# Two-input subtractions to VectorE, casts to GpSimd, in an attention and gated-convolution kernel on one Trainium2 core

## The chip, the cores and the metric

The kernel runs on one core of a Trainium2 chip. A core has a matrix engine (TensorE, PE in the rows), a vector engine (VectorE, DVE), a scalar engine (ScalarE, ACT), a general engine (GpSimd, POOL) and an engine that issues transfers (SyncE, SP). They run at the same time, each through its own list of instructions in order, and wait for one another on semaphores. The metric is the device time of the whole program in microseconds (us), as the median of several runs.

## The reference

The inputs are q, k and v (4 batches, 8 heads, 768 positions, head width 64) and the weights of a feed-forward block (512 to 1024 and back). First comes attention with a bias that falls with distance, over the last 96 positions and the first 8 ones:

```python
scores = np.matmul(q, k.transpose(0, 1, 3, 2)) / np.sqrt(D) - slopes * dist
scores = np.where(is_global | is_local, scores, -1e9)
a = softmax(scores)                       # over the keys, with 1e-9 in the denominator
x = (a @ v).transpose(0, 2, 1, 3).reshape(B, S, H * D)
```

Then a feed-forward block with a gate from a convolution of three taps along the sequence:

```python
h = np.maximum(x @ w_in, 0.0)
c = sum(conv_w[t] * shifted(h, t) for t in range(3))
out = (h * sigmoid(c)) @ w_out
```

Everything is float32, but the weights and the convolution's taps come in as 64-bit floats.

## The kernel before, in words

**Units, jobs and steps.** A unit is one batch and one half of the sequence (384 positions): 8 units. Each has 4 jobs, one for each pair of heads (32 jobs, m = 0 to 31), and each job has 3 steps, one for each block of 128 queries (96 steps, s = 0 to 95). A step makes the scores of both heads (`scores`), their maxima (`maxima`, one instruction on VectorE per head that adds the table of biases, L419), the exponentials (`exps`, ScalarE, L431), and two steps later the transposes on TensorE and their copy by ScalarE (`transposes`, L463 to L470). After the last step of a job come the product with v (`values`, L479), the scaling by the sum's inverse (`mixed`: L492 on VectorE, then a split) and the input x of the feed-forward block.

**Two-part products.** The large products use a rounded float32 format (fp32r). To keep accuracy, an operand a is split: a high part is the cast of a to fp32r, and a low part is a minus the high part, also in fp32r. This happens to k and q (`prep`, from job 5 on; jobs 0 to 4 use plain float32), to the weights (`weight_high`, `weight_low`), to x (`mixed`) and to the gated activations (`split`). A cast reads one operand, a subtraction two. Which engine does which is what the change is about. Before: casts of k and q are on ScalarE in the early jobs and on VectorE later, casts of x, weights and gated activations on ScalarE; subtractions are on GpSimd, with listed exceptions on VectorE.

**Names.** In the rows `kk` holds both parts of k (the upper 64 partitions become the low part), `qh` and `ql` those of q, `xh` and `xl` those of x, `wih`, `wil`, `woh`, `wol` those of the two weight matrices, `gh` and `gl` those of the gated activations. `rk`, `rq` are k and q as loaded, `wr` is a raw weight piece, `w` a decoded one, `hbuf` holds h, `c` the convolution.

**Feed-forward.** `ffn(n)` lists the work of unit n: products with w_in (`mm1`), the convolution (`conv`: one tap on GpSimd, L561, two on VectorE, L562 and L563), the tanh of the gates, `split`, and the products with w_out of the unit before (`mm2`). `fill` deals this list out over the 12 steps of the next unit, so attention of one unit and the block of an earlier one share the engines. A unit of even number has 56 such products in its list, an odd one 40.

**Weights.** 16 pieces are turned from 64-bit to 32-bit floats by three instructions on VectorE each (`weight_bits`, L318, L320, L322), then cast, then subtracted. Small lists of chores (`chores`) hold this work; at each step `work` takes from a list until its budget in us for the step is spent (DECODE_BY_HAND, DECODE_LATER). `need` finishes pieces at once when a product wants them.

**Order.** The first 11 steps (HAND) are recorded in the order of the code. From then on a scheduler that simulates the engines sets the order on each engine, bounded by `issue_after`. After the last product, `check_weights` and `check_gates` look for inputs that would need the slower general path; that path isn't run here.

## Time and profile before

| | |
|---|---|
| median of 3 runs | 520.48 us (520.05 to 522.03) |
| the profiled execution's own time | 522.24 us |
| its span, first to last instruction | 520.5 us |
| busy: TensorE, VectorE, ScalarE, GpSimd | 467.4, 381.5, 310.8, 281.5 us |
| granted TensorE clock, mean | 0.951 |

The times of instructions in the prediction come from the profiled execution. A row of groups gives line, engine, operation, output and inputs, count, then the busy time and the mean of one in ns, then the engine's idle time just before these instructions and what ended it. A row of a timeline gives start and duration in us. Two instructions of one engine can overlap by some hundredths of a microsecond, so the sum of durations is a little more than the busy time.

### The profile page before, as it was taken

Reading aid. Unit: us, or ns where it says so; the run is one execution under the profiler, and the core shown is the slowest. Engines: PE = TensorE matmul, PEld = TensorE weight load, DVE = VectorE, ACT = ScalarE, POOL = GpSimd, SP = SyncE. Lnnn points to the kernel's source line nnn. Section 1 sums busy time; section 2 is a strip of 40 time slices with the busy share of each in tenths; the row PEclk is TensorE's granted clock in tenths of the full one; section 3 lists DMA queues with packets and bytes.
Section 4 is the critical chain, followed back from the end, with each engine's and each line's share of the span. In section 5 each row is a group of like instructions: output and inputs, shape, how many; then the busy total and the mean of one; then the engine's idle time right before and its main releaser. Section 6 shows DMA issues by size and latency. Waiting matters only on the chain.

```text
span 520.5 us, 8853 instructions
## 1 busy us (share of the span) xinstructions
PE 467.4 (90%) x3109; PEld 397.7 (76%) x3109; DVE 381.5 (73%) x825; ACT 310.8 (60%) x825; POOL 281.5 (54%) x242
## 2 busy tenths in 40 slices
...
GB/s 187 258 202 211 150 217 105 94 93 124 104 99 61 120 94 63 76 141 127 88 122 110 87 87 94 131 128 110 101 101 122 52 67 57 55 224 210 168 60 47
DMA packets 22965, 61.78 MB, mean 119 GB/s; under 512 B 3072, under 2 KB 4608, under 8 KB 22912
## 3 DMA queue, kind: packets, MB, share of 16 engines
...
q8 instruction: 26, 0.43, 0.3%
...
## 4 chain that ended last, share of the span: by engine, by line
PE 40%; DVE 32%; ACT 10%; DMA 8%; issue 5%; POOL 2%; SPq 1%; ACTq 0%; POOLq 0%; DVEq 0%
PE o L625 17%; PE h L512 8%; DVE c L562 6%; PE pv L479 6%; DVE c L563 4%; DVE s L419 4%; PE s L400 4%; DVE c L613 3%; DMA check<-in_w_out 3%; DMA check<-in_w_in 2%; DVE kk L136 2%; ACT pbuf L431 2%; DVE w L322 2%; PE t L463 2%; DVE w L318 2%
## 5 line engine op out<-in xcount | busy, mean ns | idle before, releaser
L431 ACT ACTIVATE pbuf<-s,mm 128x232 f32<-128x232 f32 (+1 forms) x192 | 82.7, 437 | 81.1 <-DVE mm L419 73.4
L419 DVE CUSTOM_DVE_ANT_0 s<-s,tab 128x232 f32<-128x232 f32 (+1 forms) x192 | 72.9, 387 | 34.5 <-PE s L400 27.1
L625 PE MATMUL o<-woh,gh 128*128 128x512 f32 x192 | 79.4, 413 | 2.6 <-ACT gh L614 2.3
L561 POOL TENSOR_SCALAR c<-hbuf,cw 128x382 f32<-128x382 f32 (+1 forms) x64 | 51.5, 811 | 53.0 <-ACT hbuf L525 38.8
L625 PE MATMUL o<-wol,gh 128*128 128x512 f32 x192 | 77.0, 401 | 0.0
L625 PE MATMUL o<-woh,gl 128*128 128x512 f32 x192 | 76.7, 400 | 0.0
L479 PE MATMUL pv<-pt,v 104*64 104x128 f32 (+2 forms) x768 | 63.0, 294 | 13.3 <-issue 5.4
L143 POOL TENSOR_TENSOR kk<-rk,kk 64x1008 fp32r<-64x1008 f32 (+1 forms) x27 | 61.8, 2289 | 18.3 <-POOL ql L145 6.2
L145 POOL TENSOR_TENSOR ql<-rq,qh 128x768 fp32r<-128x768 f32 x24 | 48.8, 2034 | 37.4 <-DVE qh L140 25.5
L479 PEld LDWEIGHTS pv<-pt,v 104*64 104x64 f32 (+2 forms) x768 | 44.9, 142 | 31.3 <-issue 14.5
L562 DVE SCALAR_TENSOR_TENSOR c<-hbuf,cw,c 128x382 f32<-128x382 f32 (+1 forms) x64 | 57.1, 903 | 15.7 <-POOL c L561 15.5
L512 PE MATMUL h<-xh,wih 128*128 128x384 f32 x252 | 61.4, 361 | 6.4 <-ACT xh L493 4.7
L563 DVE SCALAR_TENSOR_TENSOR c<-hbuf,cw,c 128x382 f32<-128x382 f32 (+1 forms) x64 | 61.7, 972 | 0.6
L463 PE MATMUL t<-ident,pbuf 128*128 128x128 f32 (+1 forms) x192 | 51.1, 290 | 9.7 <-ACT pt L470 3.1
L512 PE MATMUL h<-xl,wih 128*128 128x384 f32 x252 | 58.9, 347 | 0.0
L512 PE MATMUL h<-xh,wil 128*128 128x384 f32 x252 | 55.1, 340 | 0.0
L400 PE MATMUL s<-kk,qh 128*128 128x232 f32 (+1 forms) x162 | 44.2, 295 | 10.8 <-ACT pbuf L431 10.8
L470 ACT ACTIVATE pt<-t 128x512 f32<-128x512 f32 x80 | 47.4, 595 | 9.9 <-PE t L464 8.2
L512 PEld LDWEIGHTS h<-xh,wih 128*128 128x128 f32 x252 | 45.9, 200 | 9.0 <-ACT xh L493 5.1
L616 POOL TENSOR_TENSOR gl<-c,gh 128x1024 fp32r<-128x1024 f32 (+2 forms) x16 | 36.3, 2276 | 26.6 <-ACT gh L614 20.2
L464 PE MATMUL t<-ident,pbuf 128*128 128x128 f32 x192 | 49.6, 282 | 0.4 <-POOL pbuf L282 0.4
L494 POOL TENSOR_TENSOR xl<-rs,xh 128x384 fp32r<-128x384 f32 x32 | 36.9, 1154 | 20.7 <-ACT xh L493 16.4
...
## 6 DMA issues: line engine op xcount, KB each, us to landing
...
```

The costliest lines, as they stand in the source:

```text
L143: G.tensor_tensor(kk[64:], rk[64:], kk[64:].bitcast(F32), ALU.subtract)
L400: last_mm[s] = T.matmul(sp[j][:, c0 : c0 + n], q_[:, j * TB + i * P : j * TB + (i + 1) * P], kk[:, j * w + k0 : j * w + k0 + n], start=st, ...
L419: last_ttr[s] = V.tensor_tensor_reduce(out=sp[j][:, c0 : c0 + n], in0=sp[j][:, c0 : c0 + n], in1=tb, scale=-0.125, scalar=3.0e38, op0=ALU. ...
L431: last_exp[s] = A.activation(pb[:, j, c0 : c0 + n], sp[j][:, c0 : c0 + n], AF.Exp, bias=mm[:, j : j + 1], scale=-1.0, accum_out=sums[m][:, ...
L463: T.transpose(pt[:ka, j, 0, :], pb[:, j, c0:P], ident)
L464: T.transpose(pt[:, j, 1, :], pb[:, j, P:256], ident)
L479: T.matmul(pv[m][64 * j : 64 * j + 64, i * P : (i + 1) * P], vt[m][:n, i, c, 64 * j : 64 * j + 64], sb[:n, j, c, :], start=c == 0, stop=c ...
L512: T.matmul(ps[:, :TB], w_[:, k, fs], x_, start=part == 0 and k == 0, stop=part == 2 and k == NK - 1,)
L561: G.tensor_scalar(c, *tap(1), 1.0, ALU.mult, ALU.mult)
L562: V.scalar_tensor_tensor(c, *tap(0), c, ALU.mult, ALU.add)
L563: V.scalar_tensor_tensor(c, *tap(2), c, ALU.mult, ALU.add)
L625: T.matmul(ps, g_[:, f], w_[:, f], start=f == 0 and part == 0, stop=f == NF - 1 and part == 2,)
```

## The change

All subtractions that make a low part (of k, q, x, the weights and the gated activations) are now on VectorE. The casts that make the high parts of k, q, x and the weights are on GpSimd; the cast of the gated activations stays on ScalarE. The chores have no list for ScalarE any more: GpSimd's list gets the cast of a weight piece in the step in which its last bits are decoded, and VectorE's list gets the subtraction three places behind the front. The budgets of VectorE's list are changed, and it comes ahead of GpSimd's.

```diff
--- before.py
+++ after.py
@@ -38,12 +38,8 @@
 NATIVE = 5
 WARM = (43, 0, 16, 16, 16, 12, 8, 4, 4, 4, 4, 4)
 EARLY = 1
-K_ON_ACT, Q_ON_ACT = 13, 10
-Q_LOW_ON_DVE = (10, 12, 14)
-W_LOW_ON_DVE = (14,)
 RELU_ON_DVE = (0, 2, 2)
-SPLIT_ON_DVE = (1,)
-DECODE_BY_HAND, DECODE_LATER = (0.7, 0.4, 0.6), (0.6, 1.2)
+DECODE_BY_HAND, DECODE_LATER = (0.3, 1.2, 1.4), (1.2, 1.2)
 FIRST_LOADS = (0, 0, 1, 2)
 SHARE = (0.3, 0.5)
 AT = ((2, 4, 5, 9, 16, 25), (1, 2, 4, 6, 7, 12, 16))
@@ -130,19 +126,12 @@
             ql = p2.tile([P, 2 * TB], F32R, tag="ql", name=f"ql{m}")
             kk = p2.tile([P, 2 * w], F32R, tag="kk", name=f"kk{m}")
             qk[m] = (qh, ql, kk)
-            if m < K_ON_ACT:
-                A.activation(kk, rk, AF.Copy)
-            else:
-                V.tensor_copy(kk, rk)
-            if m < Q_ON_ACT:
-                A.activation(qh, rq, AF.Copy)
-            else:
-                V.tensor_copy(qh, rq)
+            G.tensor_copy(kk, rk)
+            G.tensor_copy(qh, rq)
         else:
             qh, ql, kk = qk[m]
-            G.tensor_tensor(kk[64:], rk[64:], kk[64:].bitcast(F32), ALU.subtract)
-            X = V if m in Q_LOW_ON_DVE else G
-            X.tensor_tensor(ql, rq, qh.bitcast(F32), ALU.subtract)
+            V.tensor_tensor(kk[64:], rk[64:], kk[64:].bitcast(F32), ALU.subtract)
+            V.tensor_tensor(ql, rq, qh.bitcast(F32), ALU.subtract)
 
     manual = tc.manual_schedule()
     manual.__enter__()
@@ -324,14 +313,13 @@
     def weight_high(i, half):
         t = wt[i, half]
         h, l = weight_planes(i)
-        A.activation(h[:, half * HF : (half + 1) * HF], t, AF.Copy)
+        G.tensor_copy(h[:, half * HF : (half + 1) * HF], t)
 
     def weight_low(i, half):
         t = wt[i, half]
         h, l = weight_planes(i)
         sl = slice(half * HF, (half + 1) * HF)
-        X = V if i * 2 + half in W_LOW_ON_DVE else G
-        X.tensor_tensor(l[:, sl], t, h[:, sl].bitcast(F32), ALU.subtract)
+        V.tensor_tensor(l[:, sl], t, h[:, sl].bitcast(F32), ALU.subtract)
 
     def check_weights():
         width = -(-NK * FF // NCHK)
@@ -490,8 +478,8 @@
         xt[m] = (xh, xl)
         x = rs.pop(m)
         V.tensor_tensor(x, pv[m], x, ALU.mult)
-        cur["mixed"] = A.activation(xh, x, AF.Copy)
-        G.tensor_tensor(xl, x, xh.bitcast(F32), ALU.subtract)
+        G.tensor_copy(xh, x)
+        cur["mixed"] = V.tensor_tensor(xl, x, xh.bitcast(F32), ALU.subtract)
 
     def ends(s):
         return s >= 0 and s % NB == NB - 1
@@ -612,8 +600,7 @@
         else:
             V.scalar_tensor_tensor(c, c, 1.0, h, ALU.add, ALU.mult)
         A.activation(gh[:, :, sl], c, AF.Copy)
-        X = V if n % 2 in SPLIT_ON_DVE and n > 1 else G
-        X.tensor_tensor(gl[:, :, sl], c, gh[:, :, sl].bitcast(F32), ALU.subtract)
+        V.tensor_tensor(gl[:, :, sl], c, gh[:, :, sl].bitcast(F32), ALU.subtract)
 
     def mm2(b, t, f):
         gh, gl = gt[b, t]
@@ -708,7 +695,7 @@
                 fn(*a)
                 k -= cost
 
-    chores = {"dve": [], "act": [], "pool": []}
+    chores = {"dve": [], "pool": []}
 
     def work(eng, budget):
         q = chores[eng]
@@ -724,12 +711,12 @@
     def piece_bits(i, half, n):
         weight_bits(i, half, n)
         if n == 2:
-            chores["act"].append((cur["s"] + 1, 0.5, piece_high, (i, half)))
+            chores["pool"].append((cur["s"], 0.7, piece_high, (i, half)))
             free_slot((i, half))
 
     def piece_high(i, half):
         weight_high(i, half)
-        chores["pool"].append((cur["s"] + 1, 1.2, piece_low, (i, half)))
+        chores["dve"].insert(3, (0, 0.56, piece_low, (i, half)))
 
     def piece_low(i, half):
         weight_low(i, half)
@@ -737,7 +724,7 @@
 
     def need(*pieces):
         while not all(p in done for p in pieces):
-            for q in ("pool", "act", "dve"):
+            for q in ("pool", "dve"):
                 if chores[q]:
                     _, _, fn, args = chores[q].pop(0)
                     fn(*args)
@@ -786,8 +773,8 @@
             if s in (4, 6):
                 conv_weights((s - 4) // 2)
             budget = DECODE_BY_HAND[min(s // 3, len(DECODE_BY_HAND) - 1)]
-            for eng in ("pool", "act", "dve"):
-                work(eng, budget if eng == "dve" else 1.3)
+            work("dve", budget)
+            work("pool", 1.3)
         else:
             if hand:
                 hand = False
@@ -823,9 +810,8 @@
             if s < len(steps):
                 budget = DECODE_LATER[min((s - HAND) // 3, len(DECODE_LATER) - 1)]
                 with tc.issue_after(last_ttr[s].ins):
+                    work("dve", budget)
                     work("pool", 1.2)
-                    work("act", 0.9)
-                    work("dve", budget)
         if s == 0:
             for k in range(len(order)):
                 chain(*order[k])
```

Since lines are taken out, the line numbers of the changed kernel are up to 14 lower: L407 is the maximum (L419 before), L133 and L134 are the subtractions of k and q, L129 and L130 their casts, L307, L309 and L311 the three decoding instructions, L322 the subtraction of a weight piece, L480 the scaling of x (L492 before), L481 and L482 its cast and subtraction, L550 and L551 two taps, L603 the subtraction of the gates.

**First place: VectorE in the steps 6 to 8**, which are in the order of the code. Before (a row `ISA s7...` is a maximum of step 7, and `mm7` is where it is put):

```order
L492 TENSOR_TENSOR rs0_400<-pv0_383,rs0_400 128x384
L439 TENSOR_SCALAR sums1_306<-sums1_306 128x6
L440 RECIPROCAL sums1_306<-sums1_306 128x6
L255 SCALAR_TENSOR_TENSOR setup_84<-setup_84 128x24
L256 TENSOR_TENSOR cw_187<-cw_187,setup_84 128x24
L322 SCALAR_TENSOR_TENSOR w2_0_429<-wr2_0_252,w2_0_429 128x512
L419 ISA s7_0_477,mm7_487<-s7_0_477,tab_169 128x232
L419 ISA mm7_487 128x1
L419 ISA s7_1_476,mm7_487<-s7_1_476,tab_169 128x232
L419 ISA mm7_487 128x1
L318 TENSOR_SCALAR w3_0_499<-wr3_0_292 128x512
L320 SCALAR_TENSOR_TENSOR w3_0_499<-wr3_0_292,w3_0_499 128x512
```

And now, from the same instruction (the scaling of x for job 0) on:

```order
L480 TENSOR_TENSOR rs0_403<-pv0_386,rs0_403 128x384
L482 TENSOR_TENSOR xl0_456<-rs0_403,xh0_455 128x384
L427 TENSOR_SCALAR sums1_301<-sums1_301 128x6
L428 RECIPROCAL sums1_301<-sums1_301 128x6
L244 SCALAR_TENSOR_TENSOR setup_84<-setup_84 128x24
L245 TENSOR_TENSOR cw_187<-cw_187,setup_84 128x24
L322 TENSOR_TENSOR wil_189<-w1_0_329,wih_188 128x512
L309 SCALAR_TENSOR_TENSOR w3_0_435<-wr3_0_287,w3_0_435 128x512
L311 SCALAR_TENSOR_TENSOR w3_0_435<-wr3_0_287,w3_0_435 128x512
L407 ISA s7_0_485,mm7_495<-s7_0_485,tab_169 128x232
L407 ISA mm7_495 128x1
L407 ISA s7_1_484,mm7_495<-s7_1_484,tab_169 128x232
```

The subtraction for x of job 0 (`xl0`) and one of a weight piece stand ahead of the maxima of step 7, and piece `w3_0` is fully decoded there; before, its decoding began behind those maxima.

**Second place: VectorE between the maxima of step 29 and step 30**, where the scheduler sets the order. Before:

```order
L563 SCALAR_TENSOR_TENSOR c0_839<-hbuf_192,cw_187,c0_839 128x382
L419 ISA s29_1431,mm29_1436<-s29_1431,tab_169 128x232
L419 ISA mm29_1436 128x1
L140 CAST qh11_1537<-rq11_1428 128x768
L439 TENSOR_SCALAR sums9_1334<-sums9_1334 128x6
L419 ISA s30_1487,mm30_1492<-s30_1487,tab_169 128x136
L419 ISA mm30_1492 128x1
L440 RECIPROCAL sums9_1334<-sums9_1334 128x6
```

And now:

```order
L601 SCALAR_TENSOR_TENSOR c0_856<-c0_856,hbuf_192 128x8x128 x2
L133 TENSOR_TENSOR kk10_1382<-rk10_1280,kk10_1382 64x816
L427 TENSOR_SCALAR sums9_1334<-sums9_1334 128x6
L603 TENSOR_TENSOR gl0_0_1446<-c0_856,gh0_0_1445 128x1024
L428 RECIPROCAL sums9_1334<-sums9_1334 128x6
L134 TENSOR_TENSOR ql10_1381<-rq10_1281,qh10_1380 128x768
L603 TENSOR_TENSOR gl0_1_1519<-c0_856,gh0_1_1518 128x1024
L482 TENSOR_TENSOR xl7_1340<-rs7_1311,xh7_1339 128x384
L480 TENSOR_TENSOR rs8_1467<-pv8_1450,rs8_1467 128x384
L133 TENSOR_TENSOR kk11_1539<-rk11_1427,kk11_1539 64x816
L407 ISA s30_1487,mm30_1492<-s30_1487,tab_169 128x136
L407 ISA mm30_1492 128x1
```

Six subtractions (for k of jobs 10 and 11, q of job 10, x of job 7, and two tiles of the gates) and five other instructions now stand between these two maxima; before there was a cast, and an addition for the sums.

**Third place: the steps 58 and 59**, in an odd unit in the middle of the run. VectorE before:

```order
L562 SCALAR_TENSOR_TENSOR c3_2693<-hbuf_192,cw_187,c3_2693 128x386
L419 ISA s58_2956,mm58_2961<-s58_2956,tab_169 128x232
L419 ISA mm58_2961 128x1
L562 SCALAR_TENSOR_TENSOR c3_2693<-hbuf_192,cw_187,c3_2693 128x386
L563 SCALAR_TENSOR_TENSOR c3_2693<-hbuf_192,cw_187,c3_2693 128x386
L419 ISA s58_2956,mm58_2961<-s58_2956,tab_169 128x232
L419 ISA mm58_2961 128x1
L563 SCALAR_TENSOR_TENSOR c3_2693<-hbuf_192,cw_187,c3_2693 128x386
L140 CAST qh21_3091<-rq21_2995 128x768
L419 ISA s59_2998,mm59_3003<-s59_2998,tab_169 128x232
L419 ISA mm59_3003 128x1
L136 CAST kk21_3093<-rk21_2994 128x1008
```

VectorE now:

```order
L133 TENSOR_TENSOR kk20_2949<-rk20_2842,kk20_2949 64x1008
L407 ISA s58_2956,mm58_2961<-s58_2956,tab_169 128x232
L407 ISA mm58_2961 128x1
L482 TENSOR_TENSOR xl17_2914<-rs17_2873,xh17_2913 128x384
L407 ISA s58_2956,mm58_2961<-s58_2956,tab_169 128x232
L407 ISA mm58_2961 128x1
L550 SCALAR_TENSOR_TENSOR c3_2693<-hbuf_192,cw_187,c3_2693 128x386
L551 SCALAR_TENSOR_TENSOR c3_2693<-hbuf_192,cw_187,c3_2693 128x386
L407 ISA s59_2998,mm59_3003<-s59_2998,tab_169 128x232
L407 ISA mm59_3003 128x1
L550 SCALAR_TENSOR_TENSOR c3_2693<-hbuf_192,cw_187,c3_2693 128x386
L407 ISA s59_2998,mm59_3003<-s59_2998,tab_169 128x232
```

The two casts (of q and k for job 21) are gone from here, and two subtractions (k of job 20, x of job 17) came in. GpSimd in the same place, before:

```order
L145 TENSOR_TENSOR ql20_2948<-rq20_2843,qh20_2947 128x768
L143 TENSOR_TENSOR kk20_2949<-rk20_2842,kk20_2949 64x1008
L445 COPY wide18_2920<-sums18_2747 128x384
L494 TENSOR_TENSOR xl17_2914<-rs17_2873,xh17_2913 128x384
L561 TENSOR_SCALAR c3_2693<-hbuf_192,cw_187 128x386 x3
L145 TENSOR_TENSOR ql21_3092<-rq21_2995,qh21_3091 128x768
L143 TENSOR_TENSOR kk21_3093<-rk21_2994,kk21_3093 64x1008
```

GpSimd now:

```order
L130 CAST qh20_2947<-rq20_2843 128x768
L129 CAST kk20_2949<-rk20_2842 128x1008
L481 CAST xh17_2913<-rs17_2873 128x384
L549 TENSOR_SCALAR c3_2693<-hbuf_192,cw_187 128x386
L433 COPY wide18_2920<-sums18_2747 128x384
L549 TENSOR_SCALAR c3_2693<-hbuf_192,cw_187 128x386
L130 CAST qh21_3091<-rq21_2995 128x768
L549 TENSOR_SCALAR c3_2693<-hbuf_192,cw_187 128x386
L129 CAST kk21_3093<-rk21_2994 128x1008
```

Each two-input subtraction of that list has become a one-input cast of the same tile; the taps of the convolution and the copy `wide` stay.

## The prediction

> **What bounds the kernel now.** First the busy times, then the shares of the chain of waits by engine:

> ```profile
> PE 467.4 (90%) x3109; PEld 397.7 (76%) x3109; DVE 381.5 (73%) x825; ACT 310.8 (60%) x825; POOL 281.5 (54%) x242
> PE 40%; DVE 32%; ACT 10%; DMA 8%; issue 5%; POOL 2%; SPq 1%; ACTq 0%; POOLq 0%; DVEq 0%
> ```

> PE looks full, but its chain share is only 40%, and DVE has 32%. The table of stretches (us; PE, PEld, DVE, ACT, POOL busy; granted clock; DMA share; GB/s) shows where each rules:

> ```profile
> 16.00:60.00 44.00, 38.59 (x304) 28.30 (x304) 35.13 (x96) 29.56 (x89) 29.32 (x25) 0.88 0.63 204
> 60.00:115.00 55.00, 37.03 (x248) 31.70 (x247) 47.37 (x95) 35.59 (x93) 36.97 (x30) 0.84 0.39 137
> 115.00:177.00 62.00, 53.38 (x349) 45.63 (x349) 53.44 (x96) 40.74 (x106) 44.22 (x28) 0.91 0.33 102
> 242.00:292.00 50.00, 46.74 (x337) 40.26 (x337) 43.85 (x88) 30.34 (x87) 29.27 (x24) 1.00 0.36 111
> 292.00:354.00 62.00, 62.00 (x413) 55.11 (x412) 44.80 (x96) 39.30 (x104) 36.75 (x29) 0.97 0.32 100
> 354.00:404.00 50.00, 46.74 (x338) 40.25 (x337) 43.35 (x88) 30.91 (x88) 29.14 (x24) 1.00 0.36 111
> 454.00:521.00 67.00, 55.66 (x257) 45.87 (x256) 29.03 (x69) 27.59 (x64) 7.96 (x9) 0.97 0.47 143
> ```

> Three regimes. In the ramp (16 to 177) DVE is the busiest engine or near it, PE idles and its clock is down to 0.84. Then two kinds of unit alternate: one with PE without a gap (62.00 of 62), one of 50 us with PE idle for 3.3 us while DVE is 87% busy. The tail from 454 on hardly uses POOL.

> Much of DVE's busy time is waiting. In the timeline, a cast alone and one beside a POOL subtraction:

> ```profile
> 256.76 0.68 DVE L136 CAST kk<-rk 128x1008 fp32r<-128x1008 f32 x1
> 268.51 0.55 DVE L140 CAST qh<-rq 128x768 fp32r<-128x768 f32 x1
> 269.19 1.84 POOL L145 TENSOR_TENSOR ql<-rq,qh 128x768 fp32r<-128x768 f32 x1 [1.86 <-PE rt L453]
> 269.30 2.28 DVE L136 CAST kk<-rk 128x1008 fp32r<-128x1008 f32 x1
> 271.50 0.61 DVE L562 SCALAR_TENSOR_TENSOR c<-hbuf,cw,c 128x386 f32<-128x386 f32 x1
> ```

> The cast of 0.68 us took 2.28: it ended 0.55 after the POOL subtraction did (269.19 + 1.84 = 271.03), so it stood still meanwhile. The groups say how common that is:

> ```profile
> L562 DVE SCALAR_TENSOR_TENSOR c<-hbuf,cw,c 128x382 f32<-128x382 f32 (+1 forms) x64 | 57.1, 903 | 15.7 <-POOL c L561 15.5
> L563 DVE SCALAR_TENSOR_TENSOR c<-hbuf,cw,c 128x382 f32<-128x382 f32 (+1 forms) x64 | 61.7, 972 | 0.6
> L613 DVE SCALAR_TENSOR_TENSOR c<-c,hbuf 128x1024 f32<-128x1024 f32 x20 | 32.3, 1632 | 2.9 <-ACT sat L592 2.9
> L136 DVE CAST kk<-rk 128x1008 fp32r<-128x1008 f32 x11 | 18.7, 1698 | 0.0
> L136 DVE CAST kk<-rk 128x816 fp32r<-128x816 f32 x8 | 14.8, 1846 | 0.0
> L140 DVE CAST qh<-rq 128x768 fp32r<-128x768 f32 x22 | 15.0, 680 | 13.7 <-PE s L400 11.9 <-DMA rq<-in_qk 1.7
> L318 DVE TENSOR_SCALAR w<-wr 128x512 int32<-128x512 int32 x16 | 14.5, 904 | 2.1 <-DMA wr<-in_w_in 2.1
> L320 DVE SCALAR_TENSOR_TENSOR w<-wr,w 128x512 int32<-128x512 int32 x16 | 14.8, 937 | 0.2
> L322 DVE SCALAR_TENSOR_TENSOR w<-wr,w 128x512 int32<-128x512 int32 x16 | 16.2, 1015 | 0.0
> L616 DVE TENSOR_TENSOR gl<-c,gh 128x1024 fp32r<-128x1024 f32 x9 | 11.0, 1219 | 4.3 <-ACT gh L614 4.3
> L492 DVE TENSOR_TENSOR rs<-pv,rs 128x384 f32<-128x384 f32 x32 | 17.1, 535 | 10.0 <-ACT rs L455 9.9
> 12.77 0.43 DVE L318 TENSOR_SCALAR w<-wr 128x512 int32<-128x512 int32 x1 [2.11 <-DMA wr<-in_w_in]
> 13.23 0.69 DVE L320 SCALAR_TENSOR_TENSOR w<-wr,w 128x512 int32<-128x512 int32 x1
> ```

> Mean less undisturbed duration gives the stall. Taps: (903 + 972 - 2 x 610) x 64 = 42 us. L613 against the 1.22 of L616 (same size): 20 x 0.41 = 8 us. Weights: 16 x (0.47 + 0.25 + 0.33) = 17 us. Casts of k: 33.5 us against at most 19 x 0.68 = 13, so 20 us or more. Together 87 us of DVE's 381.5 are stall.

> **The change part by part.** POOL loses these groups:

> ```profile
> L143 POOL TENSOR_TENSOR kk<-rk,kk 64x1008 fp32r<-64x1008 f32 (+1 forms) x27 | 61.8, 2289 | 18.3 <-POOL ql L145 6.2
> L145 POOL TENSOR_TENSOR ql<-rq,qh 128x768 fp32r<-128x768 f32 x24 | 48.8, 2034 | 37.4 <-DVE qh L140 25.5
> L616 POOL TENSOR_TENSOR gl<-c,gh 128x1024 fp32r<-128x1024 f32 (+2 forms) x16 | 36.3, 2276 | 26.6 <-ACT gh L614 20.2
> L494 POOL TENSOR_TENSOR xl<-rs,xh 128x384 fp32r<-128x384 f32 x32 | 36.9, 1154 | 20.7 <-ACT xh L493 16.4
> L334 POOL TENSOR_TENSOR wil<-w,wih 128x512 fp32r<-128x512 f32 x8 | 12.0, 1500 | 4.3 <-ACT wih L327 4.1
> L334 POOL TENSOR_TENSOR wol<-w,woh 128x512 fp32r<-128x512 f32 x7 | 9.6, 1378 | 1.8 <-ACT woh L327 1.8
> ```

> That is 205 us. It gains 102 casts, which the trace of before doesn't show on POOL. The nearest one-input rows:

> ```profile
> 263.13 0.50 POOL L445 COPY wide<-sums 128x384 f32<-128x384 f32 x1 [1.35 <-DVE sums L440]
> L218 POOL TENSOR_SCALAR tab<-setup 128x232 bf16<-128x232 f32 x2 | 0.8, 387 | 0.2
> 265.45 1.88 POOL L561 TENSOR_SCALAR c<-hbuf,cw 128x386 f32<-128x386 f32 x2 [0.27 <-ACT hbuf L525]
> 266.33 0.62 DVE L562 SCALAR_TENSOR_TENSOR c<-hbuf,cw,c 128x386 f32<-128x386 f32 x1
> 266.87 0.87 DVE L563 SCALAR_TENSOR_TENSOR c<-hbuf,cw,c 128x386 f32<-128x386 f32 x1
> ```

> From 387 ns at 232 to 500 at 384 a line rises by 0.74 ns an element: 0.79 us for q (768), 0.96 and 0.82 for k (1008, 816), 0.60 for a weight piece, 0.50 for x. Sum: 27 x 0.79 + 15 x 0.96 + 12 x 0.82 + 16 x 0.60 + 32 x 0.50 = 71 us. Below, every cast costs the 0.50 of the smallest (51 us). Above, each cast costs what the removed subtraction of the same tile did: 61.8 for k, 27 x 2.03 for q, 16 x 1.44 for weights, 36.9 for x, 177 us. I take 71, since a cast is nearest to a copy. POOL then falls to about 150 us. ACT loses the casts of x, weights and early k, q: fewer instructions, none of them ahead of anything new.

> DVE gains 114 subtractions. Between the rows of 535 ns at 384 and 1219 at 1024, a line gives 0.68, 0.95, 1.00 and 1.20 us at 512, 768, 816 and 1008. Sum: 15 x 1.20 + 12 x 1.00 (k) + 24 x 0.95 (q) + 15 x 0.68 (weights) + 32 x 0.54 (x) + 15 x 1.22 (gates) = 98 us, less 0.08 of overlap each (the cast at 269.30 ran to 271.58, the next began at 271.50): 89 us. It loses its casts, 48.5 us with their stalls, and the other stalls, 67 us.

> New stalls are the disputed cost. Removed: 87 us of stall for 205 us of subtraction, 0.42 per us. Beside a one-input POOL instruction the tap at 266.33 took 0.62 (free) and that at 266.87 took 0.87 (0.26 stall), while POOL's pair took 1.88, where two such copies would take 1.0: here POOL waited more than DVE. Bounds: 0.26 us at one cast in three, 9 us; or 0.42 x 71 = 30 us. I take 20. DVE: 381.5 - 48.5 - 67 + 89 + 20 = 375 us, by the bounds 364 to 385.

> So DVE is no emptier, but no instruction waits 1.6 us at a time.

> A wait is added: a subtraction on DVE now waits for POOL's cast, and behind it stand the next step's maxima, for which ACT's exponentials wait (in the first place of the order, `xl0` ahead of step 7). If POOL is in a tap of the convolution just then, that is up to 0.5 us more, once a job for x; k and q are prepared a job ahead and are hidden by the steps of the running job. With POOL at 150 of 520 us this meets fewer than a third of 32 jobs, 5 us of DVE, half of it in units that PE fills; it is inside the new stall's bounds. By stretch:

> Units of the 50 us kind: 16 of 128 taps (5.3 us of stall), four casts of k (4.2), three of L613 (1.2) lose 10.7; the casts at free speed go (4 x 0.68 + 4 x 0.55, less overlap, 4.3); in come 4 x (1.20 + 0.95 + 0.54) less overlap, 9.8, and new stall, 2.5. Net -2.7 in each, with PE's idle 3.3 as the ceiling. There are two and a quarter of them: **-6 us**, between 0 and -7.5. In units of 62 us PE has no gap: **0**.

> Ramp: DVE's sum is a draw there, but POOL leaves the chain where these stood in it:

> ```profile
> 134.88 4.66 POOL gl L616 x2
> 139.60 2.39 POOL kk L143
> ```

> 7.05 us become two subtractions of 1.14 and one of 1.12 on DVE: **-4 us**, between 0 (DVE has 8.6 us free in 62 there) and -12 (if weights, now ready sooner behind one another on DVE, also cut waits between 60 and 115). The early steps get more: up to the maxima of step 10 five more decoding instructions (2.5 us), four weight subtractions (2.4) and two of x (0.9), 5.8 us; I take that as repaid later, since decoding is ahead by then. **0**, up to +6.

> Tail: no moved instruction of it is on POOL before but three tiles of the gates: **0**.

> Sum: 522.24 (the profiled execution, 1.74 beyond its span) - 10 = 512. It lies 1.76 over the median of 520.48, so against the runs shown: **510.5 us**.

> **The rivals.**

> *No change.* The 50 us units are also tied by the loop from maxima to exponentials, where ACT waits for DVE. The subtractions are put between the maxima of two steps, as casts were; if this loop sets the pace, the 2.7 is kept out of the time, and the ramp draws: 520. For: DVE has 6 us of idle there even now. Against: the stalls sit directly on the chain.

> *Slower by the ramp.* DVE is at 80 and 86% from 16 to 115. The 5.8 us ahead of step 10 are not repaid, and between the maxima of steps 29 and 30 six subtractions add 0.92 x 2 + 1.14 x 2 + 0.87 + 0.46 = 5.4 us where PE waits for k and q of job 10: 522.24 + 5.8 + 5.4 - 4 (of the steady gain) - 1.76 = 527. It decides from the point where DVE is above some 92% in 16 to 60 (35.1 + 5.8 of 44 is 93%).

> *Slower by the lock.* POOL's casts stop DVE as the subtractions did, and 89 us more of two-input work can be stopped: 0.42 x 71 x 1.4 = 42 us of stall, 22 more than taken. Over 500 us, 2.2 in each 50 us unit (the gain falls to 1) and 7 in the ramp: 510.5 + 5 + 7 = 522; with casts at the subtractions' price (177 us) 0.42 x 177 = 74, 54 more, and about 535. I put the middle, 529. [...]

> *Much faster.* Waits of PE in the ramp (18 us idle from 60 to 115) go too, since a weight's subtraction takes 0.60 instead of 1.4 to 1.5: -12 there and -7: 501.

> **How the numbers follow.** Forecast 0.49 (own range 504 to 517), no change 0.18, slower by the ramp 0.16, by the lock 0.08, much faster 0.09. A measurement here tells 0.5% (2.6 us) from nothing: faster 0.58, same 0.18, slower 0.24. The range goes from 499 to 527, which leaves out the far ends of the lock and of the much faster case.

> **What would show it.** Right: taps near 0.65 us in the mean, POOL's casts at 0.5 to 1.0, DVE busy 364 to 385, POOL about 150, units of 47 to 48 us. Wrong: taps still at 0.8 and more (the lock), casts over 1.3, DVE over 92% busy from 16 to 60 and the same maxima later (the ramp), or PE gaps in the units that had none.

## The result, and the profile after

The changed kernel takes 498.27 us in the median of 4 runs (495.63 to 501.8), beside 521.25 us (520.05 to 522.44) for the kernel before: the ratio is 0.956, with an interval of 0.950 to 0.963. Its profiled execution took 495.63 us, its span is 493.9 us. The forecast was 510.5 us, with 499 to 527 as its range: the direction was right, and the gain was more than twice the forecast one. Ratios and their intervals leave out slow executions (over 1.5% above the fastest of the same kernel) and can differ from the quotient of the medians given.

Busy times and the chain of waits of the changed kernel:

```profile
PE 461.4 (93%) x3109; PEld 395.6 (80%) x3109; DVE 379.3 (77%) x898; ACT 279.9 (57%) x764; POOL 181.1 (37%) x230
PE 73%; DVE 13%; DMA 7%; ACT 3%; issue 1%; SPq 0%; POOL 0%; DVEq 0%; ACTq 0%; POOLq 0%
```

VectorE is as busy as before (379.3 against 381.5 us), but its share of the chain fell from 32% to 13%, and TensorE's rose from 40% to 73%. Whatever was won was not won in VectorE's sum.

The same stretches as in the prediction, of the changed kernel (columns as there):

```profile
16.00:60.00 44.00, 37.02 (x278) 26.88 (x279) 40.05 (x114) 19.77 (x69) 19.88 (x27) 0.84 0.73 231
60.00:115.00 55.00, 41.99 (x266) 36.68 (x264) 48.77 (x111) 27.92 (x83) 28.97 (x30) 0.82 0.37 119
115.00:177.00 62.00, 59.59 (x415) 51.11 (x415) 56.74 (x120) 39.87 (x109) 27.58 (x31) 0.99 0.34 108
242.00:292.00 50.00, 50.00 (x356) 44.16 (x352) 41.40 (x96) 31.79 (x88) 21.14 (x25) 1.00 0.37 114
292.00:354.00 62.00, 62.00 (x443) 54.55 (x442) 47.25 (x112) 38.44 (x107) 24.73 (x29) 1.00 0.35 110
```

From 16 to 60 TensorE did less than before (278 matmuls against 304) while VectorE was busier (40.05 against 35.13). From 115 to 177 it did 415 against 349, at a clock of 0.99 against 0.91. In the last two stretches it has no gap.

Stretches of equal time hold different work, so from here on both kernels are cut at equal work: at the start of the first maximum of steps 12, 48 and 95, read from the records of that instruction (each step has two; of those of the changed kernel, L407, 96 start before 208.2 us, from 7.9 to 206.5 us, which is steps 0 to 47). First the kernel before, then the changed one:

```profile
0.00:38.10 38.10, 32.48 (x302) 25.20 (x304) 25.95 (x96) 20.77 (x70) 18.01 (x42) 0.96 0.72 212
38.10:221.70 183.60, 153.56 (x1005) 130.38 (x1000) 153.20 (x295) 117.54 (x305) 126.96 (x90) 0.89 0.35 116
221.70:436.70 215.00, 208.39 (x1439) 182.39 (x1439) 168.14 (x357) 136.24 (x371) 121.27 (x98) 0.99 0.33 101
436.70:520.50 83.80, 72.96 (x374) 59.72 (x370) 34.21 (x81) 36.24 (x82) 15.27 (x14) 0.98 0.42 127
```

```profile
0.00:40.00 40.00, 36.36 (x306) 28.06 (x307) 31.54 (x106) 18.04 (x63) 15.13 (x43) 0.91 0.75 218
40.00:208.20 168.20, 148.44 (x998) 127.23 (x997) 148.24 (x329) 96.52 (x269) 80.38 (x84) 0.92 0.39 123
208.20:412.50 204.30, 204.30 (x1434) 180.14 (x1432) 159.94 (x380) 129.25 (x355) 78.26 (x92) 1.00 0.34 106
412.50:493.90 81.40, 72.35 (x376) 60.12 (x374) 39.56 (x89) 36.10 (x79) 7.34 (x11) 0.99 0.42 131
```

This is the whole account, for this pair of executions. Steps 0 to 11 got 1.9 us longer, steps 12 to 47 got 15.4 us shorter, steps 48 to 94 got 10.7 us shorter, and the end 2.4 us: 26.6 us of span. The medians differ by 23.0 us, and a second profiled execution of the changed kernel (500.3 us of span, below) lies 20.2 us under that of before; half of what it takes longer is in its first 12 steps. In the long ramp (steps 12 to 47) VectorE's busy time fell by only 5.0 us (153.2 to 148.2) and its idle time by 10.4 (30.4 to 20.0); TensorE's idle time fell by 10.2 (30.0 to 19.8) and its busy time, at a clock of 0.92 instead of 0.89, by 5.1. In the steady part TensorE had 6.6 us of gaps (215.0 - 208.4) and has none; GpSimd's busy time fell from 121 to 78.

The groups of the changed kernel that answer to those of the prediction (mean of one in ns behind the bar):

```profile
L550 DVE SCALAR_TENSOR_TENSOR c<-hbuf,cw,c 128x386 f32<-128x386 f32 x32 | 22.2, 703 | 1.7 <-POOL c L549 1.6
L551 DVE SCALAR_TENSOR_TENSOR c<-hbuf,cw,c 128x386 f32<-128x386 f32 x32 | 22.7, 722 | 0.3
L601 DVE SCALAR_TENSOR_TENSOR c<-c,hbuf 128x1024 f32<-128x1024 f32 x20 | 26.9, 1366 | 7.2 <-ACT sat L580 7.2
L134 DVE TENSOR_TENSOR ql<-rq,qh 128x768 fp32r<-128x768 f32 x27 | 28.0, 1037 | 0.1
L130 POOL CAST qh<-rq 128x768 fp32r<-128x768 f32 x27 | 26.4, 977 | 65.6 <-PE s L388 59.4 <-DMA rq<-in_qk 6.1
L129 POOL CAST kk<-rk 128x1008 fp32r<-128x1008 f32 x15 | 19.3, 1287 | 11.7 <-DMA rk<-in_qk 6.9 <-issue 2.4 <-PE s L378 2.4
L129 POOL CAST kk<-rk 128x816 fp32r<-128x816 f32 x12 | 16.2, 1347 | 8.0 <-DMA rk<-in_qk 8.0
L481 POOL CAST xh<-rs 128x384 fp32r<-128x384 f32 x32 | 23.5, 734 | 57.6 <-DVE rs L480 57.4
```

The taps fell from 903 and 972 ns to about 700 and 720, and L601 (L613 before) from 1632 to 1366. GpSimd's casts take some 98 us in all (these rows, and 7.1 + 5.7 for the weights). Adding up, over VectorE's records, duration less undisturbed duration of the same form, the stall on VectorE fell from 104 to 31 us. The two sums depend on which durations are called undisturbed (with the shortest of each form they are 134 and 62); their difference, 72 to 73 us, hardly does.

How a stall became a gap of TensorE in the ramp of the kernel before, in its timeline just ahead of step 39 (GpSimd, VectorE, TensorE), and behind it the stretches of windows (columns as above):

```profile
167.80 2.83 POOL L143 TENSOR_TENSOR kk<-rk,kk 64x1008 fp32r<-64x1008 f32 x1 [5.28 <-DVE kk L136]
168.35 4.62 DVE L613 SCALAR_TENSOR_TENSOR c<-c,hbuf 128x16 f32<-128x16 f32 x3
172.98 5.31 POOL L616 TENSOR_TENSOR gl<-c,gh 128x1024 fp32r<-128x1024 f32 x2 [1.08 <-ACT gh L614]
173.22 3.02 DVE L613 SCALAR_TENSOR_TENSOR c<-c,hbuf 128x1024 f32<-128x1024 f32 x1
176.17 0.54 DVE L492 TENSOR_TENSOR rs<-pv,rs 128x384 f32<-128x384 f32 x1
176.81 1.51 PE L479 MATMUL pv<-pt,v 128*64 128x128 f32 x10 [5.42 <-issue]
...
171.40:176.80 5.40, 0.00 (x0) 0.02 (x1) 5.40 (x7) 4.39 (x10) 4.32 (x3) 0.93 0.38 138
176.80:180.20 3.40, 3.39 (x19) 2.41 (x20) 1.68 (x6) 1.82 (x6) 3.08 (x3) 0.50 0.20 77
180.20:183.60 3.40, 3.40 (x15) 3.40 (x16) 0.93 (x4) 1.56 (x5) 2.02 (x2) 0.61 0.00 0
```

A subtraction for k and then two for the gates ran on GpSimd. Beside the first, VectorE's L613 of 16 elements (the first of the three in the row at 168.35) took 2.32 us instead of some 0.18; beside the others, the L613 at 173.22 took 3.02 us instead of some 1.25. The scaling of x (L492), which frees the only tile of the product with v, stood behind both in VectorE's list; and TensorE, whose next product needs that tile, did nothing for 5.42 us. Some 3.9 of these are the two stalls; the rest is VectorE's own work ahead of L492. TensorE's clock then stood at 0.50 to 0.61 for 6.8 us. The row names "issue" as what ended the gap, so that it was VectorE is read from the times (176.17 + 0.54 = 176.71, and 176.81), not from the row.

### The profile page after: what moved, and what is told of

It is laid out like the page before. It is cut to its first block, busy times and chain, and to the rows that moved or that the text cites. A ratio compares the mean times of both kernels' runs of the same rounds, so it can differ in the third digit from the quotient of the medians.

```text
span 493.9 us, 8868 instructions
## 1 busy us (share of the span) xinstructions
PE 461.4 (93%) x3109; PEld 395.6 (80%) x3109; DVE 379.3 (77%) x898; ACT 279.9 (57%) x764; POOL 181.1 (37%) x230
## 3 DMA queue, kind: packets, MB, share of 16 engines
q1 hardware_dynamic: 19456, 54.98, 36.2%
## 4 chain that ended last, share of the span: by engine, by line
PE 73%; DVE 13%; DMA 7%; ACT 3%; issue 1%; SPq 0%; POOL 0%; DVEq 0%; ACTq 0%; POOLq 0%
PE o L612 24%; PE h L500 20%; PE pv L467 10%; PE s L388 7%; PE t L451 4%; PE t L452 3%; DMA check<-in_w_out 3%; DMA check<-in_w_in 2%; DVE s L407 2%; PE rt L441 2%; PE warm L152 2%; DVE w L311 2%; DMA v<-in_vv 1%; DVE w L309 1%; PE s L378 1%
## 5 line engine op out<-in xcount | busy, mean ns | idle before, releaser
L419 ACT ACTIVATE pbuf<-s,mm 128x232 f32<-128x232 f32 (+1 forms) x192 | 82.9, 438 | 95.1 <-DVE mm L407 95.0
L407 DVE CUSTOM_DVE_ANT_0 s<-s,tab 128x232 f32<-128x232 f32 (+1 forms) x192 | 72.9, 388 | 36.7 <-PE s L388 34.3
L612 PE MATMUL o<-woh,gh 128*128 128x512 f32 x192 | 77.9, 406 | 2.5 <-ACT gh L602 2.5
L467 PE MATMUL pv<-pt,v 104*64 104x128 f32 (+2 forms) x768 | 61.9, 296 | 4.7 <-DVE rs L480 3.4
L467 PEld LDWEIGHTS pv<-pt,v 104*64 104x64 f32 (+2 forms) x768 | 44.9, 144 | 22.4 <-issue 9.1
L500 PE MATMUL h<-xh,wih 128*128 128x384 f32 x252 | 59.9, 353 | 0.0
L451 PE MATMUL t<-ident,pbuf 128*128 128x128 f32 (+1 forms) x192 | 49.2, 282 | 10.4 <-ACT pt L456 4.2
L130 POOL CAST qh<-rq 128x768 fp32r<-128x768 f32 x27 | 26.4, 977 | 65.6 <-PE s L388 59.4
L452 PE MATMUL t<-ident,pbuf 128*128 128x128 f32 x192 | 48.4, 277 | 0.0
L388 PE MATMUL s<-kk,qh 128*128 128x232 f32 (+1 forms) x162 | 43.2, 294 | 3.5 <-DVE kk L133 2.3
L550 DVE SCALAR_TENSOR_TENSOR c<-hbuf,cw,c 128x382 f32<-128x382 f32 (+1 forms) x64 | 43.7, 695 | 2.3 <-POOL c L549 2.1
L500 PEld LDWEIGHTS h<-xl,wih 128*128 128x128 f32 x252 | 44.2, 191 | 0.8 <-DVE xl L482 0.8
L551 DVE SCALAR_TENSOR_TENSOR c<-hbuf,cw,c 128x382 f32<-128x382 f32 (+1 forms) x64 | 44.5, 711 | 0.5
L481 POOL CAST xh<-rs 128x384 fp32r<-128x384 f32 x32 | 23.5, 734 | 57.6 <-DVE rs L480 57.4
L500 PEld LDWEIGHTS h<-xh,wil 128*128 128x128 f32 x252 | 44.3, 190 | 0.0
```

What stands on the lines that cost most here:

```text
L388: last_mm[s] = T.matmul(sp[j][:, c0 : c0 + n], q_[:, j * TB + i * P : j * TB + (i + 1) * P], kk[:, j * w + k0 : j * w + k0 + n], start=st, ...
L407: last_ttr[s] = V.tensor_tensor_reduce(out=sp[j][:, c0 : c0 + n], in0=sp[j][:, c0 : c0 + n], in1=tb, scale=-0.125, scalar=3.0e38, op0=ALU. ...
L419: last_exp[s] = A.activation(pb[:, j, c0 : c0 + n], sp[j][:, c0 : c0 + n], AF.Exp, bias=mm[:, j : j + 1], scale=-1.0, accum_out=sums[m][:, ...
L451: T.transpose(pt[:ka, j, 0, :], pb[:, j, c0:P], ident)
L452: T.transpose(pt[:, j, 1, :], pb[:, j, P:256], ident)
L467: T.matmul(pv[m][64 * j : 64 * j + 64, i * P : (i + 1) * P], vt[m][:n, i, c, 64 * j : 64 * j + 64], sb[:n, j, c, :], start=c == 0, stop=c ...
```

## The experiments

**The theory** at the start: VectorE's stall sets the time, and each moved subtraction is worth the stall that it caused. **The rivals**: what counts is the place of a subtraction (who waits for its low part), not the sum; the pace of decoding is the gain; and, later, the half clock of TensorE is a cost of its own.

All times of stretches come from one profiled execution of each kernel, cut as above at steps 12, 48 and 95:

| kernel | ratio to before, interval | 0-11 | 12-47 | 48-94 | rest |
|---|---|---|---|---|---|
| before | 1 | 38.1 | 183.6 | 215.0 | 83.8 |
| the change | 0.956 [0.950, 0.963] | 40.0 | 168.2 | 204.3 | 81.4 |
| the change again | 0.954 [0.951, 0.958] | 43.3 | 169.7 | 204.3 | 83.0 |
| kq_back | 0.963 [0.956, 0.970] | 43.1 | 170.5 | 207.4 | 83.4 |
| gates_back | 0.977 [0.970, 0.984] | 42.5 | 177.8 | 204.9 | 84.0 |
| x_back | 0.972 [0.964, 0.979] | 44.9 | 171.8 | 205.2 | 87.6 |
| weights_back | 0.938 [0.930, 0.946] | 39.8 | 162.3 | 204.6 | 84.2 |
| weights_back_again | 0.940 [0.936, 0.944] | 38.5 | 163.1 | 204.5 | 83.6 |
| kq_alone | 0.973 [0.965, 0.980] | 36.2 | 180.1 | 204.3 | 88.7 |
| gates_alone | 0.982 [0.974, 0.990] | 36.1 | 176.6 | 211.4 | 83.9 |
| x_alone | 0.966 [0.957, 0.974] | 42.4 | 175.0 | 209.1 | 84.1 |
| weights_alone | 0.999 [0.995, 1.002] | 45.5 | 172.5 | 214.9 | 86.2 |
| old_pace | 0.946 [0.938, 0.954] | 35.8 | 170.8 | 204.3 | 81.0 |
| x_on_scalar | 0.944 [0.938, 0.950] | 42.3 | 164.0 | 203.5 | 81.5 |
| both_on_scalar | 0.945 [0.938, 0.952] | 42.4 | 168.1 | 203.5 | 84.4 |
| extra_two | 0.998 [0.995, 1.001] | 42.4 | 186.9 | 209.3 | 83.5 |
| extra_one | 1.046 [1.040, 1.053] | 42.3 | 194.1 | 230.9 | 78.6 |
| dve_early | 0.963 [0.957, 0.969] | 43.1 | 174.5 | 204.1 | 82.5 |
| dve_late | 0.952 [0.945, 0.959] | 42.4 | 168.5 | 202.9 | 84.0 |
| warm_ramp | 0.956 [0.949, 0.963] | 43.1 | 166.1 | 204.2 | 82.5 |

One caution for all of them: the scheduler that sets the order from step 11 on plans anew for each kernel, so an edit also moves other instructions of the ramp. In the steady part this matters little, as the equal 204 us of most rows show. The profiled execution of `x_alone` (512.96 us) lies above its median (510.38 us), so its stretches add up to more than its ratio says.

### One part of the change undone

In `kq_back` the casts of k and q go back to ScalarE and VectorE and their subtractions to GpSimd; in `gates_back` the subtraction of the gates, but for units of odd number from 3 on, as before; in `x_back` the cast of x to ScalarE and its subtraction to GpSimd; in `weights_back` both operations of the weights, with the old budgets and lists. The core of each edit:

```diff
-            G.tensor_copy(kk, rk)                                  # kq_back
+            if m < 13: A.activation(kk, rk, AF.Copy)
+            else: V.tensor_copy(kk, rk)
-            V.tensor_tensor(kk[64:], rk[64:], kk[64:].bitcast(F32), ALU.subtract)
+            G.tensor_tensor(kk[64:], rk[64:], kk[64:].bitcast(F32), ALU.subtract)
-        V.tensor_tensor(gl[:, :, sl], c, gh[:, :, sl].bitcast(F32), ALU.subtract)   # gates_back
+        X = V if n % 2 == 1 and n > 1 else G
+        X.tensor_tensor(gl[:, :, sl], c, gh[:, :, sl].bitcast(F32), ALU.subtract)
-        G.tensor_copy(xh, x)                                       # x_back
-        cur["mixed"] = V.tensor_tensor(xl, x, xh.bitcast(F32), ALU.subtract)
+        cur["mixed"] = A.activation(xh, x, AF.Copy)
+        G.tensor_tensor(xl, x, xh.bitcast(F32), ALU.subtract)
-        G.tensor_copy(h[:, half * HF : (half + 1) * HF], t)        # weights_back
+        A.activation(h[:, half * HF : (half + 1) * HF], t, AF.Copy)
...
```

> The changed kernel with the part for k and q undone: casts on ScalarE and VectorE by job, subtractions on GpSimd, as before. Theory A (the gain is the stall of VectorE that two-input GpSimd instructions caused; the subtractions of k and q stood for 63 of the 104 us of stall): stall goes from 31 us back to 80 to 95, and the time from 498 to 510-516. Theory B (the gain is that low parts come sooner, where a product waits for them): k and q are prepared a job ahead, so little is lost, 498-503, whatever the stall does.

> The changed kernel with the subtraction of the gated activations back on GpSimd for units 0, 1 and the even ones. Theory A: these stood for 16 of the 104 us of stall, so +3 to +5 us: 501-503. Theory B: in the chain before, two such subtractions stood one behind the other for 4.66 us with that of k behind them, and products wait for them in each of five units: +7 or more, 505-510.

> The changed kernel with x as before: its cast on ScalarE, its subtraction on GpSimd. Theory A: these stood for 10 of the 104 us of stall, so +2 to +3: 500-501. Theory B: the product with w_in needs x at once, and a subtraction of 1.01 us or more on GpSimd in place of 0.54 on VectorE delays it 32 times: +4 or more, 502-506.

> The changed kernel with the weights as before: casts on ScalarE, subtractions on GpSimd, the old lists and the old decoding budgets. Theory A: these subtractions stood for 8 of the 104 us of stall: +1 to +3, 499-501. Theory C (the ramp's gain comes from decoding more weights per step): the ramp up to step 45 loses half or more of its 14 us, 505-510.

Measured medians: 505.44, 511.0, 509.7 and 491.79 us, beside 524.91 us before. VectorE's stall by the same sum as above: 86, 41, 38 and 38 us (31 in the change). So the stall does not rank them: k and q bring back 55 us of stall and cost 0.7% (its interval overlaps that of the change, so even this is not sure), the gates bring 10 us and cost 2.1%, x 7 us and 1.5%, and the weights 7 us with a *gain* of 1.8%. The theory that the stall's sum sets the time falls. The rival, the place, put k and q, x and the gates in the right order, but each time at too low a price (503, 506 and 510 us at most); the gain of the weights was expected by neither. Where it went, for the gates (stretches of `gates_back`):

```profile
42.50:220.30 177.80, 151.86 (x1005) 130.04 (x1005) 146.78 (x322) 98.59 (x268) 91.70 (x91) 0.89 0.36 114
220.30:425.20 204.90, 204.90 (x1434) 180.62 (x1434) 160.19 (x373) 128.86 (x354) 89.96 (x98) 1.00 0.34 106
```

Most of it is in steps 12 to 47 (177.8 against 168.2), with VectorE no busier (146.8 against 148.2) and idle for 31.0 instead of 20.0 us. TensorE is idle there for 25.9 us instead of 19.8. The steady part keeps 204.9: there GpSimd's subtractions of the gates fit. In the changed kernel TensorE has no gap of over 0.5 us between 130 us and step 48, where the kernel before had the one of 5.42 us; `x_back` has one of 3.46 us there, at 171.4 us before a product with v that waits for VectorE, and `gates_back` five between 173 and 181 us, 4.0 us in all. The rest of what `x_back` costs lies mostly in the first 12 steps (44.9 us) and after step 95 (87.6 us). k and q are the only part whose return shows in the steady stretch (207.4).

### One part alone, on the kernel before

The edits are the same four parts of the change's diff, each put into the kernel before by itself.

> From the kernel before, k and q alone are changed (casts on GpSimd, low parts on VectorE). Theory A (the parts add up: each is worth what its undoing cost): 0.7% faster than before, 518 to 521 us, although VectorE's stall falls by 50 us or more. Rival B (the parts share one cause, a full GpSimd, and the first that empties it brings most): 2 to 3.5% faster, 506 to 514 us.

> From the kernel before, the gates alone are changed (all low parts on VectorE). Theory A (the parts add up): 2% faster than before, 510 to 515 us, with VectorE's idle time up to step 48 below the 42 us of before. Rival B (shared cause; k, q and x still fill GpSimd): within 1% of before, 519 to 525 us.

> From the kernel before, x alone is changed (cast on GpSimd, low part on VectorE). Theory A (the parts add up): 1.5% faster than before, 512 to 518 us. Rival B (shared cause; the cast of x queues behind k's and q's subtractions on GpSimd): within 0.7% of before or slower, 520 to 530 us.

> From the kernel before, the weights alone are changed (cast on GpSimd, low part on VectorE, new decode pace). Theory A (the parts add up: undoing them made the change faster by 1.8%): 1 to 2% slower than before, 527 to 533 us. Rival B (it takes 10 us of subtraction off GpSimd, and so helps before while it hurts the change): 0 to 1% faster, 517 to 523 us.

Measured medians: 510.07, 513.41, 510.38 and 522.91 us, beside 522.84. The parts are not additive: alone k and q, the gates and x bring 2.8, 1.8 and 3.4%, 8% together (by the medians 2.4, 1.8 and 2.4%, 6.6% together), where the whole change brings 4.4%. The rival (one cause, a full GpSimd) was right for k and q, which bring three to four times what their undoing cost, and wrong for x and the gates, which it left with nothing. For the weights the 1 to 2% slower of the adding up did not come. The stretches say why; of `kq_alone`:

```profile
36.20:216.30 180.10, 154.90 (x1006) 133.24 (x1003) 149.92 (x304) 108.66 (x294) 106.78 (x94) 0.88 0.38 119
216.30:420.60 204.30, 204.30 (x1432) 180.97 (x1431) 161.25 (x360) 136.29 (x370) 96.99 (x97) 1.00 0.35 106
```

In the steady part k and q alone reach the 204.30 us of the whole change, with TensorE full; x alone brings 5.9 of these 10.7 us, the gates 3.6, the weights nothing. There is a floor, and whoever comes second finds less to win. In steps 12 to 47 the order is the reverse: the weights alone bring 11.1 us, x 8.6, the gates 7.0, k and q 3.5. That is 30 us together, and the change has 15.4; the weights also lose 7.4 us before step 12 and 2.4 us after step 95, so that next to nothing is left of theirs.

### The pace of decoding, and the cast of x on ScalarE

```diff
-DECODE_BY_HAND, DECODE_LATER = (0.3, 1.2, 1.4), (1.2, 1.2)     # old_pace
+DECODE_BY_HAND, DECODE_LATER = (0.7, 0.4, 0.6), (0.6, 1.2)
-        G.tensor_copy(xh, x)                                     # x_on_scalar
+        A.activation(xh, x, AF.Copy)
```

> The changed kernel with the decoding budgets of before (0.7, 0.4, 0.6 and 0.6, 1.2), all engines as in the change. Theory C: weights come later and the ramp up to step 45 loses half of its 14 us or more: 505-510. Theory A: the ramp is bound by the sum of VectorE's work, not by its order: within 2 us, 497-500.

> The changed kernel with the cast of x on ScalarE again (0.52 us) and its subtraction on VectorE. GpSimd's cast of x took 0.73 us in the mean, of which 0.23 is waiting for VectorE. If that wait sits where a product needs x: 1 to 4 us faster, 494-497. If it is hidden: 498.

Measured: 496.17 us (493.68 to 502.09) and 494.26 us (493.18 to 496.19). The pace is not the gain: with the old budgets the time is the same within the interval, and the first 12 steps take 35.8 us instead of 40.0 and 43.3. The cast of x is as good on ScalarE as on GpSimd or a little better; what the change needs of x is the subtraction on VectorE.

### Both together, and the weights a second time

`both_on_scalar` joins `weights_back` and `x_on_scalar`.

> From the changed kernel: weights go back to where they were (cast on ScalarE, low part on GpSimd, old decode pace), and the cast of x goes to ScalarE with its low part on VectorE. Theory A (span = about 453 us of TensorE work at full clock, plus TensorE's idle time, plus half of the time that it works at half clock; both parts can be undone independently, -6.5 us and -4 us against the change's 498): 488 to 492 us, with idle 22 to 26 us and 12 to 15 us lost to the half clock. Rival B (ScalarE, which gets 16 + 32 casts, makes the exponentials late): 496 to 502 us, with more idle in the stretch up to step 48 than the change's 25 us.

Measured: 496.34 us (493.33 to 500.18). The expected 488 to 492 did not come. The time lies at the edge of the rival's range, but the rival's reason is not it: up to step 48 TensorE is idle for 24.7 us, as in the change (23.4 and 25.1 in its two executions), and the steady part is 203.5 us, so ScalarE makes nothing late. The ramp took 168.1 us, as in the change. Two gains of the ramp did not add up.

To tell the weights' gain from the spread between sets of runs, the change and `weights_back` ran again side by side:

> The changed kernel itself, beside the next one and the same runs of the kernel before. Both theories: 0.95 to 0.96 of before, 496 to 501 us.

> The changed kernel with the weights and the decode pace as before. Theory A (moving the weights costs the change time in its ramp, since GpSimd's queue then holds 16 casts and VectorE 16 subtractions more): 0.935 to 0.945 of before, 1 to 2% under the changed kernel beside it. Rival B (the weights are worth nothing either way, as alone on the kernel before, and the earlier 491.8 us was the spread between runs): 0.95 to 0.96 of before, within 0.7% of the changed kernel.

Measured: 500.72 us (496.62 to 502.1) and 491.62 us (488.51 to 494.83), beside 523.38 before: 0.954 and 0.940, with intervals that lie apart. So moving the weights, together with the new budgets, does cost the change 1.5%, although the same move alone costs the kernel before nothing. How much of it is the budgets is not settled: `old_pace`, which has the old budgets and everything else of the change, has a ratio (0.946) between these two, with an interval that overlaps that of `weights_back`. It reached step 48 after 206.6 us, the change after 208.2 and 213.0, `weights_back` after 202.1 and 201.6. The ramps of both second executions:

```profile
43.30:213.00 169.70, 150.33 (x1007) 128.72 (x1007) 149.98 (x329) 96.52 (x268) 78.41 (x83) 0.92 0.38 120
```

```profile
38.50:201.60 163.10, 141.44 (x991) 122.36 (x988) 149.96 (x321) 101.08 (x276) 86.73 (x86) 0.95 0.42 132
```

4.8 us come in the first 12 steps and 6.6 in steps 12 to 47, at the same VectorE busy time (149.96 and 149.98) and 6.6 us less idle time. `weights_back` has the lowest medians of this study.

### More work on GpSimd

Unused instructions on GpSimd, three after each preparation of k and q, 81 in all, once with two inputs and once with one:

```diff
+            for _ in range(3):                                   # extra_two
+                G.tensor_tensor(spare[:, :512].bitcast(BF16), qh[:, :256].bitcast(F32),
+                                qh[:, 256:512].bitcast(F32), ALU.subtract)
+            for _ in range(3):                                   # extra_one
+                G.tensor_copy(spare, qh[:, :640].bitcast(F32))
```

> The changed kernel with three more two-input GpSimd subtractions (128x256, some 0.8 us each) per job from job 5 on, 81 in all, of tiles that are there; nobody uses what they write. Theory A: they add some 65 us to GpSimd, which has 310 us free, but stop VectorE for 0.4 us per us of theirs, so its stall rises from 31 by 20 to 35 us and the time by 5 to 8, to 503-507. Theory B: nothing that a product needs comes later by more than the odd 0.8 us: 498-501.

> The same with three one-input casts of the same length (128x640, some 0.7 us) in the same places. If one-input work hardly stops VectorE: stall rises by 5 to 9 us and the time by 0 to 2, 498-500. If the number of inputs does not matter and only GpSimd's time does: the same as with the two-input ones.

The two groups, of `extra_two` and of `extra_one`:

```profile
L138 POOL TENSOR_TENSOR spare<-qh 128x256 bf16<-128x256 f32 x81 | 83.4, 1029 | 1.1
```

```profile
L138 POOL CAST spare<-qh 128x640 uint8<-128x640 f32 x81 | 78.8, 972 | 1.1
```

Measured: 522.69 us (ratio 0.998) and 548.0 us (1.046); both expectations were far too low. Two things follow. First, work with one input stops VectorE about as much as work with two: by the stall that falls beside these instructions, 19.7 us for 78.8 us of one-input work (0.25 per us) and 23.7 us for 83.4 us of two-input work (0.28). Second, GpSimd is busy for no more than half of the span (51% and 46%) and still can't take this work for nothing: 19 to 26 us are lost in steps 12 to 47. In `extra_one`, TensorE's waits name low and high parts that came late:

```profile
PE s L392 <- DVE ql L136: 16.2, 11, 5.2
PE s L392 <- POOL qh L132: 9.6, 4, 7.1
```

In the change these two (L388, L134 and L130 there) are 0.3 us and nothing. Casts of q stand behind spare work in GpSimd's list, and the score products wait for them. Why the one-input work cost 26.6 us in the steady part and the two-input work only 5.0 is not settled: the scheduler placed them differently, and no run separates the order from the work.

### More work on VectorE, early or late

Unused casts on VectorE, one in each of 32 steps:

```diff
+        if 12 <= s < 44:                                         # dve_early; dve_late: 52 <= s < 84
+            with tc.issue_after(last_ttr[s].ins):
+                V.tensor_copy(spare.rearrange("p (a b) -> p a b", a=4), tab[:, 0:4, 0:160])
```

> From the changed kernel: 32 unused casts on VectorE (128 x 640, an estimate of 0.35 to 0.7 us each, so 11 to 22 us in all), one after the second maximum of each of steps 12 to 43. Theory A (VectorE sets the pace in the ramp, up to about step 45): the time grows by the whole of it, one for one, and by some half clock on top: 510 to 525 us. Rival B (only lateness of single low parts counts, not VectorE's sum): under 4 us more, 498 to 502 us.

> From the changed kernel: the same 32 casts, one in each of steps 52 to 83. Theory A (from step 48 on TensorE has no gap left, and VectorE has 8 to 15 us to spare in each unit of 50 to 62 us): no more than 2 us, 496 to 500 us, and steps 48 to 95 take 204 to 206 us as in the changed kernel. Rival B (the units are still paced by VectorE): 11 to 22 us more, 509 to 520 us.

The group of `dve_early` with the ramp and the steady part behind it, then the steady part of `dve_late`:

```profile
L416 DVE CAST spare<-tab 128x640 uint8<-128x640 bf16 x32 | 21.4, 668 | 0.0
...
43.10:217.60 174.50, 150.66 (x1009) 129.34 (x1008) 164.64 (x361) 97.22 (x268) 76.62 (x84) 0.91 0.36 116
217.60:421.70 204.10, 204.10 (x1433) 179.93 (x1432) 160.03 (x378) 128.88 (x355) 77.21 (x92) 1.00 0.35 106
```

```profile
210.90:413.80 202.90, 202.90 (x1430) 179.38 (x1430) 174.71 (x412) 129.34 (x355) 76.86 (x92) 1.00 0.35 107
```

Late, 20 us of casts on VectorE (174.7 against 159.9 busy in the row) cost nothing: 499.12 us, 0.952. This is the clearest answer of the study: in steps 48 to 94 TensorE sets the time in the changed kernel, and no saving on VectorE can be worth anything there. Early, 21.4 us cost some 5 to 6 us of the ramp (174.5 against 168.2 and 169.7) and 505.04 us in all: neither one for one nor nothing. VectorE's busy time rose by 15 to 16 us, and its idle time, 9.9 instead of some 20 us, took most of that. The ramp is bound by chains through several engines, in which VectorE is one member.

### The half clock of the ramp

168 unused bf16 matmuls ahead of score products, in steps 15 to 35:

```diff
+            if s < 36:
+                for _ in range(8):
+                    T.matmul(sp[0][:, :P], tab[:, 0, :P], tab[:, 1, :P], start=True, stop=True)
```

> From the changed kernel: 8 unused bf16 matmuls of 128 columns (0.11 to 0.26 us each; 168 in all, some 18 us at full clock) ahead of the score matmuls of each of steps 15 to 35, into the same PSUM tile, which the score matmuls overwrite. Theory A (the half clock of the ramp, 14 us lost in the changed kernel, costs time of its own): the dips of the clock after step 15 go, the spare work lies in idle time, and the time falls to 486 to 494 us. Rival B (the half clock only stretches TensorE's work into time in which it would wait for VectorE anyway): the dips go, the time stays or grows by what does not fit into the 20 us of idle: 497 to 508 us.

```profile
L373 PE MATMUL s<-tab 128*128 128x128 bf16 x168 | 12.9, 219 | 4.0 <-ACT pbuf L422 3.9
43.10:209.20 166.10, 152.56 (x1175) 130.60 (x1176) 148.98 (x329) 96.84 (x268) 76.84 (x83) 0.97 0.39 122
```

The clock of the ramp rose from 0.92 to 0.97, and steps 12 to 47 took 166.1 us, 2 to 4 less than in the change. The whole time was 499.92 us (497.77 to 503.38), no change. The rival holds: most of the half clock only stretched TensorE's work into time in which it would have waited. That half clock follows the gaps, and filling them with spare work won nothing back; the spare work took TensorE 12.9 us itself, so a small cost of its own is not ruled out.

## Why the prediction was wrong

By its own steps, in their order.

- **VectorE's sum: right.** 375 us were forecast (364 to 385), 379.3 measured. (Its terms count 113 of the 114 subtractions that it names, which is about 1 us.) Of the stall of 31 us, 21 fall beside the new casts of q, k, x and weights, where 20 were taken (9 to 30). The stall removed was larger than the 87 us of the prediction (104), because instructions that it had left out were stopped too: the sums of the softmax (6), the 1008- and 16-element forms of L613 (5) and the casts of q (3).
- **GpSimd about 150 us: too low.** 181 measured. Its casts take some 98 instead of 71 us, since some of them last far longer than the rest: the cast of q has a mean of 977 ns, and the median one, close to the shortest (820), 832; during the seven of over 1.1 us VectorE was busy for 97 to 100% of the time.
- **Units of 50 us, -6 with -7.5 as ceiling, and units of 62 us, 0: mis-sized.** The steady part gave 10.7 us. The mechanism was right, and TensorE's gaps were the right measure: the 6.6 us of them between steps 48 and 95 all went. Left out was what can follow a gap. The rows of the kernel before for steps 48 to 59 and 60 to 71 show it, a dozen without gaps and one with 3.1 us of them:

```profile
221.70:275.40 53.70, 53.58 (x380) 47.09 (x378) 39.07 (x87) 31.85 (x91) 35.45 (x28) 1.00 0.39 117
275.40:333.50 58.10, 54.95 (x367) 48.00 (x368) 48.66 (x98) 37.78 (x99) 29.91 (x25) 0.97 0.29 94
```

  The dozen with gaps ran at 0.97: 58.10 x 0.03 = 1.7 us more. It is one piece of half clock of 3.4 us from 292.1 us on, behind a gap of 2.33 us; a gap of 2.32 us at 400 us had none behind it, so the length of a gap alone does not give this term. The prediction had quoted the same piece itself, as the 0.97 of its unit of 62 us "without a gap", and priced it at nothing. The other 2.4 us of the 10.7 are in TensorE's busy time (208.39 - 204.30 = 4.1, less 1.7); part of that is five more matmuls inside the cut.
- **Ramp, -4 (0 to -12): the step that failed.** Steps 12 to 47 gave -15.4 us. The premise, "DVE's sum is a draw there", was true (-5.0 us), and the conclusion drawn from it was wrong. The prediction then counted only the two rows in which GpSimd itself stood in the chain (7.05 us), as if a subtraction on GpSimd cost time only where the chain names GpSimd. At 168 to 177 us of the kernel before three subtractions on GpSimd had their part in a gap of 5.42 us (some 3.9 of it stall), where the chain goes over VectorE (L613), ScalarE and TensorE and doesn't name GpSimd. VectorE's idle time in these steps fell by 10.4 us, and `gates_back` brings back that idle time (31.0 us) and not the busy time. What stood in the prediction as a far bound (-12, waits of TensorE that go too) was passed, in the second execution too (183.6 - 169.7 = 13.9 us). How the 15.4 us divide among the single waits is not worked out; one gap of them is followed above.
- **Early steps, 0 (to +6): wrong by 2 to 5 us.** They are not repaid within the first 12 steps: +1.9 us in one execution, +5.2 in the other. With the old pace in `old_pace` they are gone (35.8 us), without any gain of the whole that can be measured.
- **Weights at no cost: wrong.** Undoing this part, with its budgets, makes the change 1.4 to 1.8% faster in two sets of runs.
- **Tail, 0:** -2.4 us in one execution, -0.8 in the other; no cause was looked for.
- **The sum.** For the profiled execution: forecast 512, measured 495.63; the difference of 16 is 11 in the ramp, 5 in the steady part and 2 in the tail, less 2 in the early steps.

The rivals. *Much faster* (501 us, chance 0.09) had the right mechanism: waits of TensorE in the ramp went, -13.5 us up to step 48 where it had -12 (-8.7 in the second execution). Its reason for it, the faster subtractions of weights, does not hold: with the weights undone the ramp is shorter still (162.3 us). *Slower by the ramp* came true as far as it went: VectorE is at 91% from 16 to 60 (40.05 of 44), just under its point of 92%, and the early steps lost time; but what came later was larger. *No change*, by the loop from maxima to exponentials: no, TensorE has no gap in the steady part. *Slower by the lock*: GpSimd's one-input work does stop VectorE, 0.25 us for each us in `extra_one`; it was less than the 0.42 of that rival, and the subtractions of VectorE did not raise it. The prediction's lower bound for one-input work (9 us of stall beside 71 us of casts, 0.13 per us), taken from a single tap of 0.87 us, was too low: `extra_one` shows 0.25 per us.
